# Two edits at the ends of a planned attention and gMLP kernel: the order of the first two layer norms, and programs without a block

## The chip, the cores and the metric

The kernel runs on one core of a Trainium2 chip. Its time is counted in microseconds on the device. The core has five engines with a program each: PE (matmuls; its weight loads are shown as PEld), DVE (vector), ACT (activations), POOL (general purpose) and SP, which here only issues DMAs. Semaphores tie the programs together.

## The reference

Two branches work on the same normalised input and are added to it:

```python
xn = _layernorm(x, axis=-1)                       # x: 2048 x 512
return x + _A_ref(xn, A_wqkv, A_wo) + _B_ref(xn, B_w_in, B_w_sp, B_b_sp, B_w_out)

def _A_ref(x, wqkv, wo):                          # 32 heads of 16, 8 keys at distance 2
    ...
    logits = einsum('bhsd,bhswd->bhsw', q, kg) * scale      # masked where idx < 0
    attn = softmax(logits)
    return einsum('bhsw,bhswd->bhsd', attn, vg) ... @ wo

def _B_ref(x, w_in, w_sp, b_sp, w_out):           # gMLP with 896 + 896 features
    z = gelu(x @ w_in)
    z2 = _layernorm(z[..., 896:])
    g = einsum('ts,bsf->btf', w_sp, z2) + b_sp
    return (z[..., :896] * g) @ w_out
```

## The kernel before

The 2048 rows of x form 16 blocks of 128 rows (index b), and four groups of 512 rows (index j). For each block b, `ln_block` makes the normalised rows: bnst (L555) and bnag (L557) on DVE give mean and variance, vpe (L559) adds the epsilon, rstd (L561) on POOL raises to the power -1/2, and norm (L563) on DVE subtracts and scales. Blocks 0 to 3 are then transposed on PE with an identity (xTr, L573) and copied out by ACT (xTe, L579, for block 0 in two halves); blocks 4 to 15 are transposed by DMAs of SP (xTd, L585).

From the transposed rows PE computes V (L598, copied by ACT in Ve, L603, and written to DRAM by POOL in Vw, L606), Q and K (L615, copied in L624), the second half of z (z2, L696, with gelu in L702 and squares in L707) and its first half (z1, L740). DVE multiplies Q with shifted copies of K (L636) and adds the products (L641), PE sums them over the head dimension (L649), and DVE and ACT compute the softmax. PE's largest step is the spatial product with w_sp (L823), which the output products (L879 and L888), one addition on DVE (L894) and a store (L899) follow.

None of these orders is written out. Every piece of work is a task with an engine, a cost (`est`), a priority (`prio`; smaller goes first) and dependences that come from what it reads and writes; `after` adds tasks that have to be placed earlier. `schedule` (L121) plays the program through with these costs: each engine takes, of the tasks that could start within 40 ns (`tol`, L185) of the earliest, the one with the smallest prio. Hops between engines cost 25 to 220 ns there (`hop`, L139), and PSUM banks are handed out as they come free (`place`, L148). The result is one fixed list for each engine, which the chip then executes in order, with waits on semaphores. An edit of one dependence can therefore change the order of later work on every engine.

At the start, PE has 22 warm-up matmuls on a tile of zeros (warm, L538 to L543), ten of 512 and twelve of 128 columns. They have prio 1000, so the planner uses them to fill holes of PE's list: 16 stand ahead of the first transpose xTr0, three behind it, and three at the very end. They depend on the memset of the zeros on DVE (L494) alone.

`emit` (L254) turns the lists into programs. Each engine's list is given to a method of `block`, an `nc.Block()` that `build_kernel` opens at L387. The block starts each engine's list as a body of its own, and puts a common end behind the five bodies: a jump, a drain on each engine, and a round of semaphores that lets all engines go together. At the end of its list SP waits for the channels that write to DRAM (`sp_final`, L927 to L929). In the profile, instructions of the block's end bear L387, and those of the constructor of `nc` (constants and a first round of all engines) bear L952.

Of the kernel before, what the change touches and what calls it, by code (L numbers as in the profile page):

```python
# [36 lines left out]
class Plan:  # L37
# [213 lines left out]
                                                                     last / 1000.0))  # L251


    def emit(self, nc, block, sems, chan_sems):  # L254
        for t in self.tasks:
            for d in t.deps:
                d.used = True
        cnt = {e: 0 for e in ENGS}
        for e in ENGS:
            for t in self.order[e]:  # L260
                if t.dma is None and t.used:
                    cnt[e] += 1
                    t.count = cnt[e]
                    t.tok = (("E", e), t.count)
        ccnt = {}
        for t in self.tasks:
            if t.dma is not None:
                c = t.dma["chan"]
                ccnt[c] = ccnt.get(c, 0) + 16
                t.count = ccnt[c]  # L270
                t.tok = (("C", c), t.count)
        self.chan_totals = dict(ccnt)
        for t in sorted(self.tasks, key=lambda x: (x.start, x.idx)):
            ck = {}
            for d in t.deps:
                for k, v in d.clock.items():
                    if ck.get(k, 0) < v:
                        ck[k] = v
            if t.tok is not None:
                ck[t.tok[0]] = max(ck.get(t.tok[0], 0), t.tok[1])  # L280
            t.clock = ck

        starters = {"pe": block.tensor, "act": block.scalar, "dve": block.vector, "pool": block.gpsimd,
                    "sp": block.sync}

        def semof(key):
            return sems[key[1]] if key[0] == "E" else chan_sems[key[1]]

        def run_engine(e):
            def body(eng):  # L290
                known = {}
                for t in self.order[e]:
                    need = {}
                    dl = [d for d in t.deps if known.get(d.tok[0], 0) < d.tok[1]]
                    for d in dl:
                        k, v = d.tok
                        implied = False
                        for d2 in dl:
                            if d2 is d:
                                continue  # L300
                            c2 = d2.clock.get(k, 0)
                            if c2 > v or (c2 == v and d2.tok != d.tok):
                                implied = True
                                break
                        if implied:
                            continue
                        if need.get(k, 0) < v:
                            need[k] = v
                    for k, v in need.items():
                        eng.wait_ge(semof(k), v)  # L310
                    for d in t.deps:
                        for k, v in d.clock.items():
                            if known.get(k, 0) < v:
                                known[k] = v
                    last = t.fn(eng)
                    assert last is not None, "task %s returned no instruction" % t.name
                    if t.dma is not None:
                        last.then_inc(chan_sems[t.dma["chan"]], 16)
                    elif t.used:
                        last.then_inc(sems[e], 1)  # L320
                fh = getattr(self, "final_hooks", {}).get(e)
                if fh:
                    fh(eng)
            starters[e](body)

        for e in ENGS:
            run_engine(e)


def build_kernel(nc, A_x, A_wqkv, A_wo, B_x, B_w_in, B_w_sp, B_b_sp, B_w_out, out, report=False, emit=True):  # L330
# [54 lines left out]
    plan = Plan()  # L385

    with ExitStack() as es:  # L387
        ar = es.enter_context(nc.sbuf_tensor("arena", [128, AR], BF))
        fp = es.enter_context(nc.sbuf_tensor("fpool", [128, FR], F32))
        ps = es.enter_context(nc.psum_tensor("ps", [128, PR], F32))  # L390
        block = es.enter_context(nc.Block())
        sem_h = {e: es.enter_context(nc.semaphore("sem_" + e)) for e in ENGS if e != "sp"}

        def A(name, n, o2_=0):
            return ar[:, off[name] + o2_: off[name] + o2_ + n]

        def AC(o_, dims):
            return bass.AP(tensor=ar, offset=o_, ap=[[AR, 128]] + [list(d) for d in dims])

        def Fv(name, n, o2_=0):  # L400
            return fp[:, foff[name] + o2_: foff[name] + o2_ + n]
# [7 lines left out]
        def P(bk, n, o_=0):  # L409
            return ps[:, bk.col(o_): bk.col(o_) + n]  # L410
# [53 lines left out]
        def c_mm(n):  # L464
            return max(26.0, n / 2.4 + 2.7)

        def c_act(n, psum=True, accum=False):
            return (170.0 if psum else 205.0) + n * 0.833 + (200.0 if accum else 0.0)
# [4 lines left out]
        def c_ts(n):  # L473
            return 265.0 + n * 0.27

        T = plan.add
# [70 lines left out]


        lnr = []

        def ln_block(b):
            sl = b % 8
            xs_ = b
            xin = A("xin", 512, 512 * xs_)
            T("dve", lambda v: v.bn_stats(Fv("st6", 6, 6 * b), xin), reads=([("xin", xs_)] if b else [("xin0", 0), ("xin0", 1)]), writes=[("st6", b)],  # L555
              est=685, name="bnst%d" % b, prio=b * 0.1)
            T("dve", lambda v: v.bn_aggr(Fv("mv", 2, 2 * b), Fv("st6", 6, 6 * b)), reads=[("st6", b)],  # L557
              writes=[("mv", b)], est=178, name="bnag%d" % b, prio=-1 + b * 0.1)
            T("dve", lambda v: v.tensor_scalar(Fv("vpe", 1, b), Fv("mv", 1, 2 * b + 1), LN_EPS, None, ALU.add),  # L559
              reads=[("mv", b)], writes=[("vpe", b)], est=140, name="vpe%d" % b, prio=-1.5 + b * 0.1)  # L560
            lnr.append(T("pool", lambda g: g.tensor_tensor(Fv("rstd", 1, b), Fv("vpe", 1, b), Fv("mhalf", 1), ALU.pow),  # L561
                         reads=[("vpe", b), "mhalf"], writes=[("rstd", b)], est=550, name="rstd%d" % b, prio=0))
            T("dve", lambda v: v.tensor_scalar(A("xn", 512, 512 * sl), xin, Fv("mv", 1, 2 * b),  # L563
                                               Fv("rstd", 1, b), ALU.subtract, ALU.mult),
              reads=([("xin", xs_)] if b else [("xin0", 0), ("xin0", 1)]) + [("mv", b), ("rstd", b)], writes=[("xn", sl)], est=c_ts(512),
              name="norm%d" % b, prio=-1 + b * 0.1)
            if b < NXT:
                bk = plan.bank("xTr%d" % b)

                def tr(t):  # L570
                    last = None
                    for dc in range(4):
                        last = t.matmul(P(bk, 128, 128 * dc), A("xn", 128, 512 * sl + 128 * dc), ident, start=True,  # L573
                                        stop=True)
                    return last
                T("pe", tr, reads=[("xn", sl), "ident"], writes=[bk], est=4 * c_mm(128), name="xTr%d" % b, prio=0)
                for hf in ((0, 1) if b == 0 else (None,)):
                    d0, dn = (0, 4) if hf is None else (2 * hf, 2)
                    T("act", (lambda d0, dn: lambda a: a.activation(  # L579
                        AC(off["xnT"] + d0 * S + 128 * b, [[S, dn], [1, 128]]),  # L580
                        P(bk, 128 * dn, 128 * d0).rearrange("p (c n) -> p c n", c=dn), ACTF.Copy))(d0, dn),
                      reads=[bk], writes=([("xnT", b)] if hf is None else [("xnT0", hf)]), est=c_act(128 * dn),
                      name="xTe%d_%d" % (b, d0), prio=0)
            else:
                return dma("sp", lambda e: e.dma_start_transpose(AC(off["xnT"] + 128 * b, [[S, 4], [1, 128]]),  # L585
                                                          A("xn", 512, 512 * sl)),
                    128 * 512 * 2, ("xT", sl), reads=[("xn", sl)], writes=[("xnT", b)], name="xTd%d" % b,
                    xbar=True, prio=1)
# [163 lines left out]
        for b in range(8, NB):  # L752
# [12 lines left out]
          prio=2, after=lnr[:8])  # L765
# [158 lines left out]
        chan_sems = {c: es.enter_context(nc.semaphore("c_%d" % i)) for i, c in enumerate(chans)}  # L924
# [4 lines left out]
                eng.wait_ge(chan_sems[c], plan.chan_totals[c])  # L929
        plan.final_hooks = {"sp": sp_final}  # L930
        with nc.allow_low_precision("bf16 intermediates by design"):
            plan.emit(nc, block, sem_h, chan_sems)
    return plan

def bass_parallel_sum__sliding_local_dilated__mixer_gmlp__prompt_kernel(
# [31 lines left out]
```

## Time and profile before

| what | value |
|---|---|
| median of 3 runs | 241.27 us (240.87 to 241.4) |
| the profiled execution, its own time | 242.69 us |
| its span, first to last instruction | 239.3 us |
| mean granted clock of PE | 0.999 |
| PE busy | 234.0 us (98%), 1212 matmuls |
| DVE busy | 212.8 us (89%) |
| ACT busy | 98.1 us (41%) |
| POOL busy | 33.2 us (14%) |

The busy time of an engine is the time that its records cover. A matmul's record is longer than its distance to the next one, as matmuls are pipelined, and its end is modelled. Some records of matmuls are missing. Times of the span count from its first instruction. "q" behind an engine's name stands for its sequencer, which executes waits, jumps and DMA issues. In a list of waits, each line names who waited, for whom, and how long in total, how often and at most. In the chain of waits, each piece is the work that released the next.

### The profile page before, as it was taken

How to read it: one execution, taken by the hardware profiler on the slowest of the kernel's cores; microseconds unless marked ns; L12 is line 12 of the kernel's file. 1: busy time of each engine (PE TensorE's matmuls, PEld its weight loads, DVE VectorE, ACT ScalarE, POOL GpSimd, SP SyncE). 2: the span in 40 equal slices, each digit the busy share in tenths (PEclk: the TensorE clock that was granted, in tenths of full speed). 3: DMA queues.
4: the chain of work that ended last, by engine and by line, in shares of the span. 5: the costliest groups of instructions: out<-in, count | busy, mean ns of one | idle time of the engine just before them, and what ended most of it. 6: DMA issues, size and time to landing. Idle time of an engine off the chain costs nothing.

```text
span 239.3 us, 3165 instructions
## 1 busy us (share of the span) xinstructions
PE 234.0 (98%) x1212; PEld 112.7 (47%) x1233; DVE 212.8 (89%) x267; ACT 98.1 (41%) x144; POOL 33.2 (14%) x56
## 2 busy tenths in 40 slices
PE   7999999999999999999999999999999999999995
PEld 3555555555444444444454444444444444444444
DVE  3798889999989899999999999986898999999952
ACT  2596889899888975541112111001010100101100
POOL 2378350401383500000000000000000000000000
PEclk9999999999999999999999999999999999999999
DMA  5997969993327110004079999999999997942112
GB/s 185 364 316 145 224 151 215 208 208 76 114 108 244 62 37 10 0 8 170 0 228 320 182 245 258 267 168 294 309 344 244 282 325 244 271 141 55 22 44 66
DMA packets 77806, 42.81 MB, mean 179 GB/s; under 512 B 50129, under 2 KB 77153, under 8 KB 77793
## 3 DMA queue, kind: packets, MB, share of 16 engines
q1 hardware_dynamic: 76480, 40.13, 66.2%
q0 software_dynamic: 800, 2.11, 2.8%
q10 hardware_dynamic: 512, 0.38, 0.5%
q8 instruction: 9, 0.15, 0.2%
q14 instruction: 5, 0.03, 0.1%
HBM read 26.35 MB, written 4.21 MB: 128 GB/s over the span
## 4 chain that ended last, share of the span: by engine, by line
PE 69%; DVE 16%; POOL 7%; issue 4%; POOLq 1%; ACT 1%; DVEq 0%
PE ps L823 40%; PE ps L888 10%; PE ps L879 6%; DVE arena L641 5%; PE ps L598 5%; DVE arena L636 4%; PE ps L615 3%; POOL fpool L723 3%; DVE arena L726 2%; PE ps L696 2%; POOL fpool L561 2%; PE ps L541 2%; POOL vscr L606 1%; POOLq L387 1%; DVE arena L563 1%
## 5 line engine op out<-in xcount | busy, mean ns | idle before, releaser
L823 PE MATMUL ps<-arena 128*128 128x512 bf16 x440 | 98.6, 379 | 0.4
L823 PEld LDWEIGHTS ps<-arena 128*128 128x128 bf16 x448 | 43.7, 98 | 52.6
L831 ACT ACTIVATE arena<-ps 128x1024 bf16<-128x1024 f32 (+1 forms) x16 | 14.7, 917 | 104.4 <-PE ps L823 93.8
L636 DVE TENSOR_TENSOR arena<-arena 128x4096 bf16<-128x4096 bf16 x16 | 36.6, 2285 | 0.2
L851 DVE TENSOR_TENSOR arena<-arena 128x4096 bf16<-128x4096 bf16 x16 | 36.5, 2284 | 0.0
L854 DVE TENSOR_TENSOR arena<-arena 128x2048 bf16<-128x2048 bf16 (+1 forms) x32 | 30.5, 953 | 0.4
L615 PE MATMUL ps<-arena 128*128 128x512 bf16 x126 | 28.5, 379 | 0.1
L641 DVE TENSOR_TENSOR arena<-arena 128x4096 bf16<-128x4096 bf16 x12 | 27.5, 2288 | 0.2
L888 PE MATMUL ps<-arena 128*128 128x512 bf16 (+2 forms) x116 | 26.8, 366 | 0.2
L696 PE MATMUL ps<-arena 128*128 128x448 bf16 x128 | 26.0, 352 | 0.0
L740 PE MATMUL ps<-arena 128*128 128x512 bf16 x109 | 24.2, 379 | 0.2
L615 PEld LDWEIGHTS ps<-arena 128*128 128x128 bf16 x128 | 14.5, 113 | 13.0
L894 DVE TENSOR_TENSOR arena<-ps,arena 128x512 bf16<-128x512 f32 (+2 forms) x17 | 11.2, 657 | 9.4 <-PE ps L888 9.4
L624 ACT ACTIVATE arena<-ps 128x1024 bf16<-128x1024 f32 x16 | 16.2, 1019 | 4.3 <-PE ps L615 3.6
L696 PEld LDWEIGHTS ps<-arena 128*128 128x128 bf16 x128 | 12.4, 98 | 11.5
L888 PEld LDWEIGHTS ps<-arena 128*128 128x128 bf16 x119 | 11.6, 98 | 12.7
L740 PEld LDWEIGHTS ps<-arena 128*128 128x128 bf16 x112 | 10.8, 98 | 12.7
L746 ACT ACTIVATE arena<-ps 128x1024 bf16<-128x1024 f32 (+1 forms) x16 | 14.1, 916 | 6.1 <-PE ps L740 6.1
L879 PE MATMUL ps<-arena 128*128 128x512 bf16 (+2 forms) x67 | 16.5, 366 | 0.1
L702 ACT ACTIVATE arena<-ps 128x896 bf16<-128x896 f32 x16 | 14.6, 913 | 2.8 <-PE ps L696 2.6
L598 PE MATMUL ps<-arena 128*128 128x512 bf16 x60 | 14.9, 379 | 0.4 <-ACT arena L579 0.2
L707 ACT ACTIVATE arena<-arena 128x896 bf16<-128x896 bf16 x16 | 15.2, 949 | 0.2
(56 smaller groups left out, 176.4 us busy)
## 6 DMA issues: line engine op xcount, KB each, us to landing
arena<-vscr SPq DMA_DIRECT2D x16, 1024.0 KB, 6.8
arena<-in_A_x_dram SPq DMA_DIRECT2D x29, 128.0 KB, 5.3
vscr<-arena POOLq DMA_DIRECT2D x16, 128.0 KB, 2.8
out_dram<-arena SPq DMA_DIRECT2D x15, 128.0 KB, 5.1
arena<-in_A_wqkv_dram SPq DMA_DIRECT2D x2, 512.0 KB, 6.6
arena<-in_B_w_in_dram SPq DMA_DIRECT2D x2, 448.0 KB, 5.2
arena<-in_B_w_in_dram SPq DMA_DIRECT2D x1, 896.0 KB, 5.3
arena<-in_B_w_out_dram SPq DMA_DIRECT2D x1, 896.0 KB, 5.5
```

Source lines behind the costliest of these rows:

```text
L598: last = t.matmul(P(bk, 512), AC(off["xnT"] + dc * S + 128 * b, [[1, 128]]), AC(off["wv"] + 512 * dc, [[1, 512]]), start=(dc == 0), stop=( ...
L615: last = t.matmul(P(bk, 512, 512 * which), AC(off["wqk"] + 2048 * which + 512 * dc + c, [[4, 128]]), AC(off["xnT"] + dc * S + 512 * j, [[1 ...
L624: T("act", lambda a: a.activation(AC(qo, [[ko - qo, 2], [1, 512]]), P(bk, 1024).rearrange("p (t n) -> p t n", t=2), ACTF.Copy, scale=0.5), ...
L636: T("dve", (lambda pbv, qb, kb: lambda v: v.tensor_tensor(pbv, qb, kb, ALU.mult))(pbv, qb, kb), reads=rd, writes=[("pb", s_)], est=c_tt(40 ...
L641: T("dve", (lambda av, bv: lambda v: v.tensor_tensor(av, av, bv, ALU.add))(av, bv), reads=[("pb", 1)], writes=[("pb", acc)], est=c_tt(4096 ...
L696: last = t.matmul(P(bk, 448, 512 * hf), AC(off["xnT"] + dc * S + 128 * b, [[1, 128]]), AC(off["w_in2"] + 896 * dc + 448 * hf, [[1, 448]]), ...
L740: last = t.matmul(P(bk, 512, 512 * i), AC(off["w_in1"] + 896 * dc + 128 * fc, [[1, 128]]), AC(off["xnT"] + dc * S + 512 * j, [[1, 512]]), ...
L823: last = t.matmul(P(bk, 512, 512 * i), AC(off["z2"] + FH * sh + 128 * fc, [[1, 128]]), AC(off["wT%d" % r_] + sh * 512, [[1, 512]]), start= ...
L851: T("dve", lambda v: v.tensor_tensor(tv, tv, av, ALU.mult), reads=[("attn", b)], writes=[("Vs", sv)], est=c_tt(4096), name="pv%d" % b, pri ...
L854: T("dve", (lambda n: lambda v: v.tensor_tensor(A("Vs", n, 4096 * sv), A("Vs", n, 4096 * sv), A("Vs", n, 4096 * sv + n), ALU.add))(n), wri ...
L879: last = t.matmul(P(bk, cn), AC(off["OT"] + 512 * tb + 128 * cc, [[1, 128]]), AC(off["wo"] + 512 * cc + c0, [[1, cn]]), start=(cc == 0), s ...
L888: last = t.matmul(P(bk, cn), AC(off["z1T"] + fc * S + 128 * tb, [[1, 128]]), AC(off["w_out"] + 512 * fc + c0, [[1, cn]]), start=False, sto ...
```

## The change

Two edits are made together. First, bnst1, the statistics of block 1, gets an `after` on norm0, the normalisation of block 0: the planner may place it on DVE only behind norm0. A list `norms` collects the tasks for it. Second, `nc.Block()` is gone: `emit` writes each engine's list with `nc.tensor`, `nc.scalar`, `nc.vector`, `nc.gpsimd` and `nc.sync` straight behind what the constructor of `nc` left in that engine's program. There are no bodies to jump to, and no common end; each engine's program ends with its last task, and SP's with the waits of `sp_final`.

```diff
-    def emit(self, nc, block, sems, chan_sems):
+    def emit(self, nc, sems, chan_sems):
...
-        starters = {"pe": block.tensor, "act": block.scalar, "dve": block.vector, "pool": block.gpsimd,
-                    "sp": block.sync}
+        engines = {"pe": nc.tensor, "act": nc.scalar, "dve": nc.vector, "pool": nc.gpsimd, "sp": nc.sync}
...
-            starters[e](body)
+            body(engines[e])
...
-        block = es.enter_context(nc.Block())
...
         lnr = []
+        norms = []
...
             T("dve", lambda v: v.bn_stats(Fv("st6", 6, 6 * b), xin), ...
-              est=685, name="bnst%d" % b, prio=b * 0.1)
+              est=685, name="bnst%d" % b, prio=b * 0.1, after=([norms[0]] if b == 1 else ()))
...
-            T("dve", lambda v: v.tensor_scalar(A("xn", 512, 512 * sl), xin, Fv("mv", 1, 2 * b),
+            norms.append(T("dve", lambda v: v.tensor_scalar(A("xn", 512, 512 * sl), xin, Fv("mv", 1, 2 * b),
...
-            plan.emit(nc, block, sem_h, chan_sems)
+            plan.emit(nc, sem_h, chan_sems)
```

More of the change, by code (lines that the diff above doesn't have):

```diff
@@ L562, in ln_block @@
                          reads=[("vpe", b), "mhalf"], writes=[("rstd", b)], est=550, name="rstd%d" % b, prio=0))
-            T("dve", lambda v: v.tensor_scalar(A("xn", 512, 512 * sl), xin, Fv("mv", 1, 2 * b),
+            norms.append(T("dve", lambda v: v.tensor_scalar(A("xn", 512, 512 * sl), xin, Fv("mv", 1, 2 * b),
                                                Fv("rstd", 1, b), ALU.subtract, ALU.mult),
               reads=([("xin", xs_)] if b else [("xin0", 0), ("xin0", 1)]) + [("mv", b), ("rstd", b)], writes=[("xn", sl)], est=c_ts(512),
-              name="norm%d" % b, prio=-1 + b * 0.1)
+              name="norm%d" % b, prio=-1 + b * 0.1))
             if b < NXT:
```

## The prediction

> **What bounds the kernel now.** The page comes first. It counts PE busy for 234.0 of 239.3 us, DVE for 89%, ACT for 41%, and the granted clock is full in every slice. A busy PE may still be waiting between matmuls, so the second view is the list of waits, cut to the time from 14 us on and to PE's weight loads:
>
> ```profile
> engine line waited for: us in total, times, longest us
> PEld ps L649 <- DVE arena L641: 1.2, 2, 0.6
> ```
>
> From 14 us to the end PE waits for somebody at two places only, both in the logits (L649), both for the sums on DVE (L641). The 1.2 us are idle time of the weight loads; PE itself, which still works off the last matmuls, stands about 0.1 us each time. Matmul starts agree: back to back at full clock a 512-column matmul follows the last after 0.22 us (the row of L598 below: four in 1.04 us, each recorded as 0.38 long, so (1.04-0.38)/3), and the stream keeps that pace. Between 7.28 us and the last matmul of the product I find some 0.5 us in which PE could have run and did not: 0.14 at 9.3, 0.08 at 11.2, and about 0.1 at each of the two L649 waits, the rest in scraps. PE's program is therefore a solid block: when its first real matmuls start earlier, everything does; nothing inside it can be saved. So the third view is the chain of waits from 3 to 10 us (start, length, what):
>
> ```profile
> 2.71 3.63 PE ps L541 x13
> 6.34 0.48 PE ps L573 x4
> 6.82 0.02 issue
> 6.84 0.39 ACT arena L579
> 7.24 0.05 issue
> 7.28 1.04 PE ps L598 x4
> ```
>
> L541 are the warm-up matmuls on zeros. The chain runs through them, not through the normalisation. The timeline of DVE and PE shows why (start, length, engine, line, operation):
>
> ```profile
> 4.51 0.56 POOL L561 TENSOR_TENSOR fpool<-fpool 128x1 f32<-128x1 f32 x1 [2.93 <-DVE fpool L559]
> 5.13 0.69 DVE L555 BATCH_NORM_STATS2 fpool<-arena 128x6 f32<-128x512 bf16 x1 [0.71 <-DMA arena<-in_A_x_dram]
> 5.75 0.40 DVE L563 TENSOR_SCALAR arena<-arena,fpool 128x512 bf16<-128x512 bf16 x1
> 1.25 5.09 PE L541 MATMUL ps<-arena 128*128 128x512 bf16 x16 [1.25 <-DVE arena L494]
> 6.20 0.61 PE L573 MATMUL ps<-arena 128*128 128x128 bf16 x4
> 6.60 0.47 PE L541 MATMUL ps<-arena 128*128 128x128 bf16 x3
> ```
>
> rstd0 is ready at 5.07, but DVE has bnst1 in front of norm0, whose data land only at 5.11. norm0 thus starts at 5.75 instead of 5.10. Meanwhile PE works through 16 warm-ups. Its last one holds the array until about 6.13 (5.09 us of records end at 6.34; the last is 0.31 long and the next may follow 0.11 after its start). The transpose xTr0 starts at 6.20.
>
> The end is the other place, the sequencers' records of lines 929 and 387:
>
> ```profile
> L929 SPq EVENT_SEMAPHORE  x4: 28/28/1965, 236.7 to 238.9; - x4
> ...
> L387 SPq COMPARE_BRANCH  x1: 41/41/41, 238.9 to 238.9; - x1
> L387 SPq DRAIN  x1: 13/13/13, 239.1 to 239.1; - x1
> L387 SPq EVENT_SEMAPHORE  x1: 17/17/17, 239.3 to 239.3; - x1
> ```
>
> SP's last wait for a store ends at 238.9; then come a jump, a drain and a round through POOL, and all engines are let go at 239.3.
>
> **1. The common end goes: -0.4 us.** The jump starts at 238.94, its 0.04 us carry SP's fifth and last wait, and that wait stays as a semaphore instruction of about the 0.03 us of its four neighbours: SP would end at 238.97. The span ends at 239.34 now. Nothing covers these 0.37 us. Outside the span lie 242.69-239.3 = 3.4 us, which the trace doesn't show. PE, DVE, ACT and POOL would reach them at 236.9, 237.1, 237.7 and 84.6 instead of 239.3; if some of their closing work then passes while SP waits, up to 1 us more could go (my bound: less than a third of the 3.4, as most of it must lie before the start or behind SP). A loss has no row that would carry it. I take 0.
>
> [...]
>
> **2. No jump at the start: -0.1 us.** Behind the first barrier SP starts its first DMA 0.06 us after its semaphore instruction, POOL 0.10, DVE its memset 0.17. Elsewhere the next instruction follows such an instruction after 0.03 to 0.05. So a jump costs 0 to 0.12. PE's stream hangs on DVE's memset (L494), so I go by DVE: 0.1; the ends are 0 and -0.12.
>
> **3. norm0 ahead of bnst1: -0.15 us, between 0 and -0.65.** norm0 itself moves from 5.75 to 5.10. But PE executes in program order, and the planner still puts 16 warm-ups ahead of xTr0. By the costs in the code rstd0 ends at plan time 5238, norm0 may start at 5298 and ends at 5701 (5716 before), and xTr0 is ready at 5761. At 5705 PE is free, 5761 is more than the 40 of tolerance away, and the sixteenth warm-up goes first, as before. In this execution xTr0 could thus start at 6.13 instead of 6.20: -0.06. Only if the warm-ups ran faster would norm0 count in full. Their pace, 0.11 us for 128 columns, is half that of the transposes at 8.15 (four in 0.39, 0.22 each: 0.057), so the clock opened in between, at about 7 us. An execution in which it opens earlier gets up to 0.65. I take -0.15, nearer to the profiled one.
>
> [...]
>
> **4. What the planner moves with it: +0.15 us, between 0 and +0.36.** bnst1 now follows norm0: bnag1, vpe1, rstd1, norm1 come 0.1 later (norm1 at 7.20 instead of 7.10). In plan time norm1 ends at 7842 (7147 before), V0's matmuls at 7533. In this hole the planner puts the three warm-ups that stood behind the last product at the end, where they cost nothing (after L888, beside the last DVE addition). On the chip there is no hole: V0 ends at about 8.1, norm1 at 7.6. Three matmuls of 0.057 are +0.17. Next, norm2 falls behind bnst3 in the plan (8855 against 8768, over 40 apart), xTr2 so behind V1, and V1 starts right after z2_0's first half: it must wait for xTe1, which ACT can't start before Ve0 has left at about 8.8, and 0.59 us later: PE stands about 0.19 us. In return the waits of 0.14 and 0.08 vanish. Sum 0.17+0.19-0.22 = 0.14.
>
> The further moved steps have cover. bnst3 ahead of norm2 waits for x3, landed at 7.93, and ends at 8.6, when rstd2 is there too (8.5): norm2 at 8.6, needed by xTr2 at 10.3. bnst4 ahead of norm3 waits for x4, landed at 9.55: norm3 ends at 10.6, xTr3 comes up at about 12.5. norm4 comes earlier, as POOL no longer has Vw2 ahead of rstd4, so the first transposing DMA may leave SP a microsecond or more before its 13.95; SP's loads are all issued by 11.7, and the transposes stay behind them.
>
> **5. The rest of the plan: 0, between -0.1 and +2.3.** From about 17 plan us on, DVE has the same work behind it as before, 0.2 us later by the plan and 0.2 us earlier by the durations above. PE has slack except at L649.
>
> Sum: -0.4-0.1-0.15+0.15 = -0.5. The profiled execution would take 242.2 instead of 242.69. It lies 1.4 above the median of the runs; none of the terms belongs to that difference, so I take the same -0.5 off the median: 241.27-0.5 = 240.8.
>
> **Rivals.** (a) *The plan shakes PE.* At L649 PE already waits for L641's sums, with no slack, and a delay of DVE against PE goes through one to one. One DVE operation moved ahead of a sum costs 0.69 (bnst) to 2.29 (a product, L636). The point from which it decides is 0.5 us: beyond it the change loses. With one statistic of 0.69 the time is 241.5, with a product 243.1. For it: every plan order behind the edit is open. Against it: the planner keeps PE full by nearly the same costs that the trace shows. Chance 0.26: 0.18 slower by over 0.2%, 0.08 within. (b) *The start takes more:* clock open early or the engines' early end paying outside the span, another -0.4 to -1: 239.8 to 240.4. Chance 0.16. [...] Chance 0.13, within. (d) The forecast, 240.5 to 241.1, chance 0.45. It straddles the bound of 0.2% (0.48 us, about what a measurement of this kernel can tell from no change): 0.34 below, 0.11 within.
>
> Faster 0.34+0.16 = 0.50; within 0.08+0.13+0.11 = 0.32; slower 0.18. The range reaches down to rival (b)'s end, 239.8, and up into (a), 241.9, past its 0.69 case; the product case, about a tenth, and tails stay out.
>
> **What would show it.** Right: no L387 line and a span that ends with SP's L929 near 238.9 less the gain; norm0 near 5.1, xTr0 hardly before 6.0; three L541 between L598 and L573, none at the end; L649 still the only PE wait after 14 us. Wrong: xTr0 at 5.5 (step 3 too small), any new PE wait after 14 us (rival a), or a time outside the span other than 3.4 (step 1).

## The result and the profile after

| | before | after |
|---|---|---|
| median of the runs | 241.40 us (9 runs, 240.87 to 241.90) | 240.06 us (9 runs, 239.42 to 241.12) |
| ratio | | 0.9939, 95% interval 0.9922 to 0.9955 |
| profiled execution, its own time | 242.69 us | 239.45 us |
| its span | 239.3 us | 238.0 us |

The kernel is 1.3 us faster; the forecast was 0.5. The sign and the range were right, the size was not, and the time fell into rival (b). Lines of the changed kernel stand one or two lines earlier than those of before: L539 are its warm-ups, L572 the transposes, L597 V, L695 z2, L648 and L640 the logits and the sums that they wait for, L928 SP's last waits.

The chain of waits from 3 to 10 us in the changed kernel (start, length, what):

```profile
2.71 3.09 PE ps L539 x13
5.80 0.24 PE ps L572 x4
6.04 0.02 issue
6.07 0.39 ACT arena L578
6.46 0.05 issue
6.50 1.04 PE ps L597 x4
7.54 0.17 PE ps L539 x3
```

V starts at 6.50 instead of 7.28, still behind the warm-ups, and the three leftover warm-ups stand behind V, as step 4 had it. The timeline of DVE and PE shows the two starts (start, length, engine, line):

```profile
1.25 4.55 PE L539 MATMUL ps<-arena 128*128 128x512 bf16 x16 [1.25 <-DVE arena L492]
5.64 0.39 PE L572 MATMUL ps<-arena 128*128 128x128 bf16 x4
...
5.15 0.41 DVE L562 TENSOR_SCALAR arena<-arena,fpool 128x512 bf16<-128x512 bf16 x1 [0.68 <-POOL fpool L560]
5.48 0.69 DVE L554 BATCH_NORM_STATS2 fpool<-arena 128x6 f32<-128x512 bf16 x1
```

norm0 runs ahead of bnst1 and ends at 5.56; the transpose starts at 5.64. But the same 16 warm-ups take 4.55 us here and took 5.09 before. The ten of 512 columns start 0.40 to 0.43 us apart in both. Here the next one follows after 0.24, and those of 128 columns then every 0.056; before it was 0.43 and 0.107. So PE's pace doubled at about 5.1 us in this execution and at about 6.9 before, where the trace has its first clock record: full clock from 6.87 us on, and nothing recorded ahead of it. The recorded texts call this moment the opening of the clock; the trace of after has no clock record, and its pace alone shows it. So one pair of profiles can't say what the edit did at the start. The waits of PE's weight loads from 14 us on, and SP's last waits:

```profile
PEld ps L648 <- DVE arena L640: 0.7, 2, 0.5
```

```profile
L928 SPq EVENT_SEMAPHORE  x5: 17/28/28, 237.7 to 238.0; - x5
```

The wait at the logits fell from 1.2 to 0.7 us, and the span ends with SP's waits. One line of the page had been passed over: the chain that ended last, by engine. First before, then after:

```profile
PE 69%; DVE 16%; POOL 7%; issue 4%; POOLq 1%; ACT 1%; DVEq 0%
```

```profile
PE 98%; issue 1%; DVE 0%; ACT 0%
```

Before, nearly a quarter of the chain ran through DVE and POOL. After, it runs through PE alone. How much of the chain leaves PE differs between executions: in the eight profiles with the order of before PE has 63 to 87%, in the six with the new order 95 to 98%.

### The profile page after: what moved, and what is told of

Same layout as the page of the kernel before. It is cut to its first block, busy times and chain, and to the rows that moved or that the text cites. A ratio compares the mean times of both kernels' runs of the same rounds, so it can differ in the third digit from the quotient of the medians.

```text
span 238.0 us, 3156 instructions
## 1 busy us (share of the span) xinstructions
PE 233.0 (98%) x1211; PEld 112.2 (47%) x1233; DVE 213.3 (90%) x267; ACT 97.6 (41%) x144; POOL 32.4 (14%) x56
## 3 DMA queue, kind: packets, MB, share of 16 engines
q0 software_dynamic: 800, 2.11, 2.7%
## 4 chain that ended last, share of the span: by engine, by line
PE 98%; issue 1%; DVE 0%; ACT 0%
PE ps L822 40%; PE ps L614 12%; PE ps L695 10%; PE ps L887 10%; PE ps L739 10%; PE ps L597 6%; PE ps L878 6%; PE ps L539 2%; PE ps L648 1%; PE ps L572 0%; ACT arena L578 0%; DVE arena L893 0%; DVE arena L492 0%
## 5 line engine op out<-in xcount | busy, mean ns | idle before, releaser
L640 DVE TENSOR_TENSOR arena<-arena 128x4096 bf16<-128x4096 bf16 x12 | 27.5, 2289 | 0.2
L695 PE MATMUL ps<-arena 128*128 128x448 bf16 x128 | 26.0, 352 | 0.0
L695 PEld LDWEIGHTS ps<-arena 128*128 128x128 bf16 x128 | 12.4, 98 | 11.5
L597 PE MATMUL ps<-arena 128*128 128x512 bf16 x60 | 15.3, 379 | 0.5 <-ACT arena L578 0.3
```

The source lines that it names most:

```text
L597: last = t.matmul(P(bk, 512), AC(off["xnT"] + dc * S + 128 * b, [[1, 128]]), AC(off["wv"] + 512 * dc, [[1, 512]]), start=(dc == 0), stop=( ...
L640: T("dve", (lambda av, bv: lambda v: v.tensor_tensor(av, av, bv, ALU.add))(av, bv), reads=[("pb", 1)], writes=[("pb", acc)], est=c_tt(4096 ...
L695: last = t.matmul(P(bk, 448, 512 * hf), AC(off["xnT"] + dc * S + 128 * b, [[1, 128]]), AC(off["w_in2"] + 896 * dc + 448 * hf, [[1, 448]]), ...
```

## The experiments

Two theories of the end and two of the order stood against each other. A: the common end costs 0.36 us of the span and nothing outside it; B: it costs more outside. C: up to the logits DVE sets the pace and PE waits; D: PE is one solid block. The logits (L649) come in four groups, one for each 512 rows, at about 48, 75, 99 and 123 us. PE stands ahead of the second and the third; what e7's expectation calls the first logits sum is the second group's. "Outside" below is a run's time less its own span, as the median over the runs. The kernel before ran beside each group on the same chip: 241.42 us with e1 to e4, 241.60 with e5 to e8, 241.51 with e9 to e12.

**e1, the kernel before again.**

> The kernel before, unchanged, for the spans of its runs: the changed kernel's runs lie 1.4 to 2.1 us above their spans, the one profiled execution of before 3.4 us above its span. Theory A (the end pays in the span alone, 0.36 us, and the rest of the 1.34 us is the earlier start of PE's matmuls): the runs of before lie about 1.5 us above their spans too, and the 3.4 us was one execution. Theory B (without a common end the part outside the span shrinks as well): they lie about 3 us above it in every run. Time: 241.4, ratio 1.000 within 0.002 by both.

Measured: 241.52 us, ratio 1.0005 (0.9990 to 1.0021); outside 2.21 us, median span 239.25. The changed kernel's own runs have 1.52 outside and a median span of 238.6. The 3.4 of the profiled execution was an exception, and yet 0.7 us go outside the span. Both theories had the number wrong: before, A said 1.5 and B 3 outside. That the end costs nothing outside the span is excluded; the 0.7 is half of what B said. This profile also shows that norm0 is not always late before (DVE; start, length, line):

```profile
4.34 0.68 DVE L555 BATCH_NORM_STATS2 fpool<-arena 128x6 f32<-128x512 bf16 x1
5.11 0.41 DVE L563 TENSOR_SCALAR arena<-arena,fpool 128x512 bf16<-128x512 bf16 x1
```

Here x1 had landed at 3.83 instead of 5.11, bnst1 was through before rstd0 was there, and norm0 started at 5.11, as early as the edit makes it. Of the eight profiles with the order of before, four have x1 at 3.7 to 3.8 and one at 4.6, and in all these norm0 starts at 5.07 to 5.24; three have it at 5.1 to 5.5 and norm0 at 5.75 to 6.11.

**e2, the edge alone.**

```diff
-              est=685, name="bnst%d" % b, prio=b * 0.1)
+              est=685, name="bnst%d" % b, prio=b * 0.1, after=([norms[0]] if b == 1 else ()))
```

> The edge from norm0 to bnst1 alone; the block with its jumps and its common end stays. Theory A: 240.4 to 240.8 (0.6 to 1.0 us less than 241.4), by first matmuls of V at 6.5 to 7.2 us instead of 7.3, and more in an execution whose PE clock opens early. Theory B, by which the end pays most: 241.0 to 241.4. Rival of both, that the planner's other order pays later than 15 us: V starts as before and PE still ends earlier.

Measured: 241.34 us, ratio 1.0000 (0.9987 to 1.0014). The median span is 0.25 us shorter than that of before (238.95 against 239.2), but 2.40 us lie outside it instead of 2.23. PE's timeline:

```profile
1.25 5.09 PE L541 MATMUL ps<-arena 128*128 128x512 bf16 x16 [1.25 <-DVE arena L494]
6.13 0.63 PE L574 MATMUL ps<-arena 128*128 128x128 bf16 x4
6.56 0.51 PE L541 MATMUL ps<-arena 128*128 128x128 bf16 x3
7.24 1.04 PE L599 MATMUL ps<-arena 128*128 128x512 bf16 x4 [0.17 <-ACT arena L580]
8.12 0.33 PE L541 MATMUL ps<-arena 128*128 128x128 bf16 x3
```

norm0 is there at 5.52, the warm-ups hold PE until 6.13, and V starts at 7.24, where it started before: step 3 of the prediction as the profile of before had it. Yet PE's last matmul of the product starts at 236.10 instead of 236.45, so something later pays (from V's first matmul to the last one it is 228.86 us instead of 229.16). Theory A's number for the edge failed; the rival, that the order pays behind 15 us, holds.

**e3, the block alone taken away.**

```diff
-        block = es.enter_context(nc.Block())
...
-            starters[e](body)
+            body(engines[e])
```

> The block is gone, the order of before stays. Theory A: 241.0 (0.37 us less: no L387 lines, the span ends with SP's last wait, PE's last matmul where it was). Theory B: 239.5 to 240.4 (1 to 1.9 us less), with a span only 0.4 us shorter and the rest outside it.

Measured: 240.36 us, ratio 0.9962 (0.9944 to 0.9980). Outside: 1.52 us. The 0.36 that the trace of before has behind SP's last wait, and 0.7 outside, make the 1.06 that the medians differ by. Theory A falls.

**e4, no block, but a common end.**

```diff
             plan.emit(nc, sem_h, chan_sems)
+        nc.all_engine_barrier()
```

> No block and no jumps, the order of before, but a drain on every engine and one round of semaphores of all engines written behind the last task: the common end without the jumps. If the jumps cost something by themselves (theory: up to 0.1 us at either end), 241.2; if only the common end counts, 241.4, the same as before within 0.1 us and against the kernel without the common end 0.3 to 0.4 us more (theory A) or 1 to 1.9 us more (theory B).

Measured: 241.23 us, ratio 0.9993 (0.9971 to 1.0015); outside 2.19. The common end brings the 0.7 back without any jump. Inside the span it takes 0.26 us from SP's last wait to the end (in the block: 0.36), so the jump at the end was worth 0.1 us. Leaving out the jump at the start was worth nothing: the first DMA of SP starts at 0.79 to 0.80 in every profile, and DVE's first memset at 0.92 both before and after the change.

**e5, e6 and e9: who is let go late.** The common end joins only some engines.

```diff
+        ET = mybir.EngineType
+        nc.multi_engine_barrier([ET.PE, ET.Activation, ET.DVE, ET.SP])   # e5
...
+        nc.multi_engine_barrier([ET.PE, ET.SP])                          # e6
...
+        nc.multi_engine_barrier([ET.Pool, ET.SP])                        # e9
```

> No block, the order of before; the drains and the semaphore round at the end join PE, ACT, DVE and SP, and POOL, which has done its last work at 85 us, ends alone. The common end of all five costs 2.2 us outside the span against 1.5 without it. If POOL is what pays outside the span (it then does its closing work 150 us early), this one lies 1.5 us outside; if any other engine is, 2.2 us.

> The same with a common end of PE and SP alone; ACT, DVE and POOL end by themselves. If PE's own closing takes longest, 2.2 us outside the span; if ACT's, DVE's or POOL's does, 1.5 us. A value between the two would mean that the engines' closings, started together, hinder each other.

> No block, the order of before, a common end of SP and POOL alone. With nobody, SP and PE, all but POOL, and all five in the common end, 1.5, 1.8, 1.8 and 2.2 us lay outside the span. If each engine that is let go late adds its own share (PE 0.3, POOL 0.4, ACT and DVE none), this one lies 1.9 us outside; if the slowest closing alone counts and that is POOL's, 2.2 us; if two late engines suffice for a fixed 0.3 us whoever they are, 1.8 us.

| held until SP is done | outside, median | runs | time | ratio (interval) |
|---|---|---|---|---|
| nobody (e3) | 1.52 us | 12 | 240.36 | 0.9962 (0.9944 to 0.9980) |
| PE (e6) | 1.82 | 9 | 240.81 | 0.9968 (0.9952 to 0.9984) |
| PE, ACT, DVE (e5) | 1.83 | 9 | 240.90 | 0.9962 (0.9943 to 0.9981) |
| POOL (e9) | 2.29 | 9 | 241.16 | 0.9980 (0.9967 to 0.9993) |
| all (e4) | 2.19 | 12 | 241.23 | 0.9993 (0.9971 to 1.0015) |

POOL alone costs as much as all five. PE costs 0.3, and with ACT and DVE it costs no more. e5 and e6 fell between the two values that their expectations had named, so e9 was needed: of the values that its three readings named, 2.2 us came closest (2.29). With POOL held, the time outside is about the same whether the others are held or not (2.19 and 2.29), and without POOL it is the same for PE alone (1.82) as for PE, ACT and DVE (1.83); the shares don't add. The differences are in the time outside (1.35 to 1.66 us in the runs of e3, 1.60 to 2.11 in e6, 1.80 to 2.45 in e5, 2.21 to 3.33 in e9); the ratios of the times overlap and don't separate e3, e5 and e6. The groups ran on three chips, where the kernel before has 2.21 to 2.23 outside. POOL's last piece of work is done at about 84 us, so without the common end its program is over about 150 us before SP's. What takes the time outside the span, on POOL or elsewhere, no trace shows.

**e7, one more matmul ahead of the logits.** It goes on e3. Its result is overwritten, so the product is the reference's.

```diff
+                    if b == 14 and hf == 0:
+                        t.matmul(P(bk, 512), AC(off["xnT"] + 128 * b, [[1, 128]]), AC(off["wv"], [[1, 512]]),
+                                 start=True, stop=True)
```

> The order of before without the block, and one more 512-column matmul (its result is overwritten) in V of block 14, some 2 us ahead of the first logits sum; the planner doesn't know of it, so all orders stay. Theory C (ahead of 75 us DVE sets the pace, PE waits 0.30 us for it at the logits): the wait shrinks from 0.30 to about 0.09 us, the stretch from the first V matmul to the last stays 229.16 us, and the time is that of the kernel without the block, 240.4. Theory D (PE is a solid block, as the prediction had it): the stretch grows to 229.37 us and the time by 0.22 us.

Measured: 240.39 us, ratio 0.9942 (0.9923 to 0.9962), e3's time, though the kernel before took 0.2 us longer here than beside e3. The waits of the weight loads from 14 us on:

```profile
PEld ps L650 <- DVE arena L642: 1.0, 2, 0.6
```

They are 0.2 less than the 1.2 of before; PE's own wait at the second group of logits shrank from 0.30 to 0.09 us. PE around it in e3, then in e7:

```profile
73.71 1.24 PE L596 MATMUL ps<-arena 128*128 128x512 bf16 x5
75.09 0.56 PE L647 MATMUL ps<-arena 128*128 128x32 bf16 x16
```

```profile
73.65 1.46 PE L599 MATMUL ps<-arena 128*128 128x512 bf16 x5
75.03 0.64 PE L650 MATMUL ps<-arena 128*128 128x32 bf16 x19
```

A record of V is 0.38 us long, so V's last matmul starts at 74.57 in e3 and 74.73 in e7; the logits follow after 0.52 and 0.30 us, where 0.22 would be the pace. The stretch from V came out at 230.06, because z2's weights landed late in this execution (8.56) and PE stood 1.03 us ahead of z2. Counted from z2's first matmul instead, it is 227.93; e5 and e6 have 228.07, and the difference of 0.14 is a wait for xTe1 that PE doesn't have when z2 comes late. The extra 0.216 us of PE work cost nothing. For work between z2 and the logits theory C holds, and D falls. D's other half stays: in the seven other profiles with the order of before, V starts anywhere from 6.43 to 7.48, and its stretch to the last matmul is 229.2 to 229.3 us in all. So DVE's pace is itself tied to the start, and a later start of V is paid in full.

**e8 and e12, fewer warm-ups in the changed kernel.** The lists of all engines stay as they are but for the warm-ups left out.

```diff
-    NWARM = 22
+    NWARM = 12      # e8; 10 in e12
...
-            n_ = 512 if wi < NWARM - 12 else 128
+            n_ = 512 if wi < 10 else 128
```

> The changed kernel with 12 warm-ups instead of 22: ten of 512 and two of 128 columns ahead of the first transpose, none behind it; all other orders stay. By theory C the three matmuls that go behind V (0.17 us) and an earlier first transpose (5.7 us instead of 5.6 to 6.1) are worth at most what the logits don't take back, 0 to 0.2 us: 239.9 to 240.1. By theory D 0.2 to 0.5 us: 239.5 to 239.9. [...]

> The changed kernel with only the ten warm-ups of 512 columns; all other orders stay. The first transpose starts when block 0 is normalised, at 5.5 to 5.6 us, whatever the clock. If the start of V is what spreads the runs of the changed kernel (239.4 to 241.1), these lie closer together and at 239.6 to 239.9. Rival: PE does less before V, its clock opens later in part of the executions, V runs at half pace there, and the runs spread as before or lie above those with twelve warm-ups (239.7).

Measured: e8 239.74 us (6 runs, 239.58 to 239.89), ratio 0.9913 (0.9895 to 0.9930); e12 239.46 us (6 runs, 239.29 to 240.20), ratio 0.9913 (0.9895 to 0.9930). PE in e12:

```profile
5.66 0.61 PE L572 MATMUL ps<-arena 128*128 128x128 bf16 x4
6.75 1.16 PE L597 MATMUL ps<-arena 128*128 128x512 bf16 x4 [0.47 <-ACT arena L578]
7.76 0.40 PE L572 MATMUL ps<-arena 128*128 128x128 bf16 x4
8.82 0.93 PE L695 MATMUL ps<-arena 128*128 128x448 bf16 x4 [0.67 <-DMA arena<-in_B_w_in_dram]
```

PE still ran at the slow pace at the transposes (0.61 us for four, where they take 0.39 at the fast one), and V started at 6.75, where it starts at 7.24 with 22 warm-ups and the slow pace at the transposes (0.63 in e2 and e10). The rival, by which PE's pace doubles later, isn't excluded by two profiles: in both it doubled at about 7.0, late but within the range with 22 warm-ups (about 4.1 to 7.2), and V's second matmul came 0.33 and 0.35 us behind the first instead of 0.23. The runs do lie closer together (0.3 and 0.9 us from the lowest to the highest, against 1.7 and 2.9 for the changed kernel, which has more runs). The times missed: e8 lies in theory D's range (239.5 to 239.9) and not in C's, and e12 lies below its own. Against the kernel before beside them the two gained 1.9 and 2.1 us, the changed kernel 1.3 and 1.4. That a start of V is passed on in full would fit, but these two profiles are the slowest of their six runs and don't show where the 0.5 to 0.7 come from. In this execution the next limit is seen: z2's weights landed at 8.78, and PE stood 0.8 us for them.

**e10, the changed kernel with a common end.**

> The changed kernel with a common end of all five engines written behind its programs. Theory: the whole gain but that of the order goes, about 2.2 us outside the span and 0.26 us more inside it, 241.0. Rival, from the edge alone with the block, which lay 2.4 us outside: the order itself adds 0.2 us outside the span once engines end together, 241.2, so the edge gains only where there is no common end.

Measured: 241.33 us, ratio 0.9999 (0.9982 to 1.0016), median span 238.7, but 2.93 us outside (2.34 to 3.66). The rival holds, and by more than it said: with a common end the new order costs outside the span at least what it gains inside. Why is open; it wasn't tried which engine's program does it.

**e11, the changed kernel again.**

> The changed kernel, unchanged, beside the one with ten warm-ups on the same chip: 240.1 (ratio 0.994). By theory C at most one short wait at the logits (0.15 us or less) after 14 us, a stretch from the first V matmul to the last of 228.9 to 229.0 us when V starts at full clock, and 1.5 us outside the span.

Measured: 240.12 us (12 runs, 239.44 to 242.31), ratio 0.9943 (0.9923 to 0.9964), outside 1.51. The stretch from V missed its number (229.60), for the reason seen in e7: V at 6.49, but the weights at 8.62. The weight loads of this kernel in the first 12 us:

```profile
PEld ps L695 <- DMA arena<-in_B_w_in_dram: 0.7, 1, 0.7
PEld ps L597 <- ACT arena L578: 0.5, 1, 0.5
```

## Why the prediction was right in sign and too small

Of the 1.3 us only the 0.36 inside the span came as forecast. The rest came by two ways that the sum had at nothing, the end outside the span and the order behind z2; that the result lies in the range is owed to the room left for rival (b), chance 0.16.

| step | forecast | measured |
|---|---|---|
| 1, common end, inside the span | -0.4 | -0.36 (0.1 of it the jump) |
| 1, common end, outside | 0, bound -1 | -0.7 |
| 2, jump at the start | -0.1 | 0 |
| 3 and 4, order up to z2 | 0.0 (-0.15 and +0.15) | +0.2 in the mean, not clear of the scatter |
| 5, order behind it | 0, bound -0.1 | -0.5 |
| sum | -0.5 | -1.4 (medians: -1.3 and -1.4) |

**Step 1** had its mechanism right inside the span, where the records gave it. "I take 0" for the outside is the larger of the two misses. The trace couldn't price it, and the bound of 1 us held it; letting the four engines end early was worth 0.7 (2.2 us outside against 1.5), and it hung on POOL (2.29 with POOL held alone) and PE (1.82 with PE held alone).

**Step 2** took the longest of three gaps for a jump. The gap of 0.17 us ahead of DVE's memset is there without a jump as well: the changed kernel's memset starts at 0.92 too.

**Step 3** was right about norm0 (5.15) and about the 16 warm-ups, and the order of PE's and DVE's lists came out as worked out by hand. But the delay that the edit takes away exists only where x1 lands after some 4.6 us, three of eight profiles, and V hangs on whichever comes later, norm0 or the end of the warm-ups, which moves with the doubling of PE's pace: V starts at 6.43 to 7.48 with the order of before, at 6.49 to 7.24 after. A warm-up of 512 columns follows the last after 0.43 us ahead of the doubling and after 0.22 behind it. The place of that change, with the warm-ups' records (4.04 us for the sixteen in e7, 4.40 in e11, 4.55, 5.09), puts the doubling between about 4.1 us (e7) and 7.2 (e10), a spread of 3.1 us. What sets the moment, no run shows.

**Step 4**: the three warm-ups behind V cost their 0.17, and V1 waits 0 to 0.2. The start of z2, behind all this, lies at 7.6 to 8.6 us in the eight profiles of the old order (mean 8.2) and at 8.0 to 8.7 in four of the new (8.4). But x1 landed late, at 4.85 to 5.11, in all four of the new, and in only three of the eight; those three have z2 at 8.4 to 8.6 (mean 8.5). So the +0.2 of the table compares unlike executions; with x1 late in both it is about -0.1, and e11's 8.7 is a late load. No gain or loss at the start is shown, and so neither the -0.15 of step 3 nor the +0.15 of step 4.

**Step 5** is the one that failed in kind. From z2's first matmul to the last one PE needs 228.0 to 228.1 us in the old order (seven profiles) and 227.4 to 227.6 in the new (four). In the old order PE waits 0.30 us at the second group of logits and 0.28 at the third; in the new one not at all and 0.14 to 0.17. I had put these waits at about 0.1 us each, because I took 0.22 of each gap for a missing record; e1, whose profile has all 1233 matmuls, shows 0.30 and 0.28 as well, and with the 0.14 and 0.08 its gaps come to 0.8 us, not 0.5. And "nothing inside it can be saved" read PE's short waits as harmless, where the page's chain said that DVE leads up to there. What saves them is DVE: the sum that the second group waits for ends 66.4 to 66.5 us after z2's start before and 65.9 to 66.1 after. The lead doesn't come from the first blocks, where bnst3 and bnst4 now stand ahead of norm2 and norm3: counted from z2's start, DVE ends bnst7 at 6.9 us in e1 and e2 alike, and norm10 at 13.3 in e1 and 13.5 in e2. It comes at blocks 10 to 13, where norm waits for POOL's rstd. DVE there in e1, then in e2:

```profile
21.01 0.41 DVE L563 TENSOR_SCALAR arena<-arena,fpool 128x512 bf16<-128x512 bf16 x1 [0.63 <-POOL fpool L768]
24.40 0.41 DVE L563 TENSOR_SCALAR arena<-arena,fpool 128x512 bf16<-128x512 bf16 x1 [0.34 <-issue]
```

```profile
21.63 0.41 DVE L564 TENSOR_SCALAR arena<-arena,fpool 128x512 bf16<-128x512 bf16 x1 [0.23 <-POOL fpool L769]
23.99 0.41 DVE L564 TENSOR_SCALAR arena<-arena,fpool 128x512 bf16<-128x512 bf16 x1 [0.16 <-POOL fpool L562]
```

These are norm10 and norm12; L768 and L769 are memsets beside which rstd10 stands in POOL's list. The new list has bnag11 and vpe11 ahead of norm10, which fill part of the wait, and norm12 ahead of bnag13. The two waits come to 1.0 us in all eight profiles of the old order and to 0.4 in the four of the new. At norm13 DVE is 0.3 ahead, at the sum 0.5. That this is the cause is read from the traces. The planner also moved early work of PE, ACT and POOL, and no kernel changed DVE's order alone. In the times the order's net share is small: without a block 240.36 (e3) against 240.06 and 240.12, with intervals that overlap.

**The rivals.** (a) didn't come: the waits at L649 became shorter. Its place was right, its sign wrong. (b) came by its second half, the early end outside the span. The case with the chance of 0.13, a time within 0.2% of before, didn't come: without the block alone (e3) the ratio is 0.9962 (0.9944 to 0.9980), with both edits 0.9939 (0.9922 to 0.9955). The version with ten warm-ups has the lowest median of all, 239.46, against 240.12 for the changed kernel on the same chip; their intervals overlap (0.9895 to 0.9930 and 0.9923 to 0.9964).

## What to carry to other kernels

Where five engines end together, look at what lies between the span and the measured time as well: an engine that is done early should be let go early, and only the one that waits for the last store need stay; here that was worth 0.7 us outside the span. Read the chain that ended last over the whole span before calling the busiest engine a solid block; a short wait of that engine, at a place that the chain enters from another engine, can mean that the other one sets the pace; look where that one waits. And profile more than one execution before pricing the first microseconds: the landing of a load (3.74 to 5.47 us for x1) and the doubling of PE's pace (4.1 to 7.2) moved them by more than the edit did.

## What the runs showed of the hardware

- Time outside the span, with the order of before, depends on which engines are held until SP is done: 1.5 us with none, 1.8 with PE, 2.2 to 2.3 with POOL.
- The moment when PE's pace doubled (from 0.43 to 0.22 us between matmuls of 512 columns) varied between about 4.1 and 7.2 us over 14 profiles of nearly the same start, and with it the length of the same 16 warm-ups (4.04 to 5.09 us).
- The load of x's block 1, issued at 1.40 to 1.43 us, landed between 3.74 and 5.47 us, and z2's first weights between 7.39 and 8.78.
- Leaving out the jump into the block moved no start (SP's first DMA at 0.79 to 0.80 us, DVE's memset at 0.92, with and without it); the jump at the end, ahead of the drain, cost 0.1 us.
